# Attention over a long cache: dealing each head's keys to partitions in runs of 512 instead of runs of 128 per piece

## The chip, the cores and the metric

One core of one Trainium2 chip. The metric is the device time of one execution in microseconds (us). Runs of one call share a chip and the runs of the kernel before. A ratio below is the mean time of one kernel's fast runs over the mean of the other's fast runs of the same rounds, so it isn't quite the ratio of the medians quoted beside it. A run counts as slow when its time is more than 1.5% above the fastest of the same kernel.

## The reference

One token attends to a cache of 65,536 keys in each of 32 heads. A small gated feed-forward network runs beside it and the two results are mixed.

```python
B, Sq, D = 1, 1, 512
H, Sk, Dh = 32, 65536, 128            # k_cache, v_cache: [1, 32, 65536, 128] bf16, 512 MB each
q = (x @ wq).reshape(B, Sq, H, Dh)    # (transposed to heads first)
scores = einsum("bhqd,bhkd->bhqk", q, k_cache) * Dh ** -0.5
o = einsum("bhqk,bhkd->bhqd", softmax(scores), v_cache)
a = o.reshape(B, Sq, H * Dh) @ wo
b = (silu(x @ w_gate) * (x @ w_up)) @ w_down
g = sigmoid((x * gate_w).sum(-1))
out = g * a + (1 - g) * b
```

## The kernel before

K and V stream once through a ring of four slots of 4 MB (32 KB in each of 128 partitions). A head of 16 MB is four pieces. `kv_src` says which bytes of the cache make up piece `i`, and in it lies the whole change.

```python
P = 128; GB = 8; CB_MAX = 128; NSLOT = 4; SHARE = 4     # CB = 128 keys per partition and piece, NCH = 4 pieces per head

def kv_src(t, i):
    h, c = divmod(i, NCH)
    return t[0, h, c * CB * P:(c + 1) * CB * P, :].rearrange("(p r) d -> p (r d)", p=P)

# ... one queue (SyncE) issues every large load, as soon as its slot is free:
def load(eng, w, job):
    i = place[job]
    if i >= NSLOT:
        for cond in free_of(jobs[i - NSLOT]):
            w(*cond)
    for n, (dst, src) in enumerate(pieces(job)):
        done = ld[i % NSLOT]
        # ...
        eng.dma_start(dst, src).then_inc(done, 16)
```

The use of a piece doesn't depend on which keys it holds. Three quarters of a K piece go through TensorE (transpose, copy by ScalarE, product with q), and one quarter through VectorE (product with a broadcast q, then a sum). A V piece is multiplied by the matching column of probabilities. The source lines named in the profile are marked.

```python
# TensorE, K:
last = nc.tensor.transpose(dst[:, k * 128:(k + 1) * 128], src[:, b * 128:(b + 1) * 128], ident[:])   # L535
# ScalarE:
nc.scalar.activation(KT[:, g % NKT, :], kt_ps(g), ACT.Copy, bias=0.0)                                # L345
# TensorE, scores:
last = mm(psS[:, c % 2, col:col + 1], KT[:, g % NKT, k * 128:(k + 1) * 128], qc[...])                # L548
# VectorE, the last quarter of the piece:
nc.vector.tensor_tensor(prod[:], kb, qb, ALU.mult)                                                   # L424
# TensorE, V: partition p and block b of V meet partition p and column b of the probabilities
last = mm(psO[:, c % 2, 0:1], src[:, b * 128:(b + 1) * 128], p_of(c)[:, b:b + 1], ...)               # L566
```

Of the kernel before, what the change touches and what calls it, by code (L numbers as in the profile page):

```python
# [5 lines left out]
P = 128  # L6
# [21 lines left out]
def bass_gated_mix__mha_block_cached__swiglu_ffn__decode_kernel(  # L28
# [21 lines left out]
    CB = min(CB_MAX, NC_H)  # L50
# [14 lines left out]
    with ExitStack() as ctx:  # L65
# [55 lines left out]

        def kv_src(t, i):
            h, c = divmod(i, NCH)
            return t[0, h, c * CB * P:(c + 1) * CB * P, :].rearrange("(p r) d -> p (r d)", p=P)

        jobs = [("wq", i) for i in range(NQW)]
        for s in range(NK):
# [27 lines left out]
        def pieces(job):  # L155

            kind, i = job
            if kind == "wq":
                return [(w_q(i), wq_dram[:, i * CQ:(i + 1) * CQ, :])]
            if kind == "wg":  # L160
                return [(by_rows(w_gate()), wg_dram)]
            if kind == "wu":
                return [(by_rows(w_up()), wu_dram)]
            if kind == "wgu":
                return [(by_rows(w_gate()), wg_dram), (by_rows(w_up()), wu_dram)]
            if kind == "wd":
                return [(w_down(), wd_dram)]
            src = kv_src(A_k_cache if kind == "k" else A_v_cache, i)
            dst = flat(job)[:, 0:CB * 128]
            if job == ("v", NK - 1):  # L170
                cut = (CB - TAIL) * 128
                return [(dst[:, 0:cut], src[:, 0:cut]), (dst[:, cut:], src[:, cut:])]
            return [(dst, src)]
# [502 lines left out]
```

## Time and profile before

| | before |
|---|---|
| time, first three runs | 2563.17 us median (2563.04 to 2563.19) |
| span in the profile | 2563.3 us |
| busy: TensorE / ScalarE / VectorE | 72% / 58% / 49% |
| load queue's packets, share of the 16 DMA engines' span | 98.8% |
| 32 KB packets, counted from the trace's DMA records | 32,768; median 1214 ns, mean 1223.8 ns |
| of these over 1273 ns | 670 |

These are lines of the profile page of the kernel before. First comes the span. The DMA and GB/s lines cut the span into 40 equal slices, with the busy share in tenths and the rate. Then come the load queue (packets, MB, share of 16 engines), the chain of work that ended last, three groups of instructions (busy us, mean ns of one, then idle time before them and what ended it), and the two kinds of large load (KB each, median us from issue to landing).

```profile
span 2563.3 us, 88371 instructions
...
DMA  9999999999999999999999999999999999999996
GB/s 403 423 425 432 432 431 431 430 431 430 433 430 432 430 431 433 430 433 429 433 429 431 433 426 431 430 432 427 426 425 418 431 429 427 423 422 426 422 419 297
...
q1 hardware_dynamic: 37874, 1083.46, 98.8%
...
DMA 67%; PE 13%; ACT 11%; issue 9%; POOL 0%; DVE 0%; ACTq 0%; SPq 0%; POOLq 0%; DVEq 0%
DMA ring<-in_A_k_cache_dram 66%; ACT KT L345 10%; PE psT L535 9%; PE psS L548 2%; PE psO L566 1%; ACT pcol L325 1%; DMA ring<-in_A_wq_dram 1%; PE psT L596 0%; PE psT L515 0%; POOL amx L304 0%; PE psS L508 0%; PE psO L589 0%; DVE mxs L441 0%; ACTq L205 0%; DVE sS L434 0%
...
L345 ACT ACTIVATE KT<-psT 128x1024 bf16<-128x1024 bf16 x1536 | 1443.0, 1039 | 972.7 <-PE psT L535 969.8
L535 PE MATMUL psT<-ident,ring 128*128 128x128 bf16 x12288 | 1138.7, 255 | 527.6 <-DMA ring<-in_A_k_cache_dram 525.5
...
L424 DVE TENSOR_TENSOR prod<-ring,qbc 128x2048 f32<-128x2048 bf16 x256 | 586.7, 2292 | 592.1 <-DMA ring<-in_A_k_cache_dram 586.7
...
ring<-in_A_k_cache_dram SPq DMA_DIRECT2D x128, 4096.0 KB, 28.0
ring<-in_A_v_cache_dram SPq DMA_DIRECT2D x127, 4096.0 KB, 33.7
```

The DMA engines are full in every slice but the last, and what the chain follows back is mostly K loads. The first instructions on a K piece (L535, L424) are idle over 500 us waiting for it. By contrast, ScalarE's idle time is spent on TensorE. So the loads bound the kernel.

A 4 MB load takes some 28 to 34 us from issue to landing, yet one completes every 4.19 MB / 430 GB/s = 9.8 us. About three are in the queue together, so the issue of a load isn't what costs.

The packet records size this. Nearly every packet is one row of 32 KB. The 5th and the 50th percentile are 1213 and 1214 ns, so there is a floor: 32,768 B / 1213 ns = 27.0 GB/s per engine, 432 GB/s for 16, within 1 GB/s of the best slice of the page (433). The Trainium skill, "HBM Reference", section "Specifications (TRN2)", says that a core streaming alone gets about 425 GB/s, bounded by its 16 DMA engines. This trace agrees, with 425 GB/s over the span.

### The profile page before, as it was taken

How to read it: one execution, taken by the hardware profiler on the slowest of the kernel's cores; microseconds unless marked ns; L12 is line 12 of the kernel's file. 1: busy time of each engine (PE TensorE's matmuls, PEld its weight loads, DVE VectorE, ACT ScalarE, POOL GpSimd, SP SyncE). 2: the span in 40 equal slices, each digit the busy share in tenths (PEclk: the TensorE clock that was granted, in tenths of full speed). 3: DMA queues.
4: the chain of work that ended last, by engine and by line, in shares of the span. 5: the costliest groups of instructions: out<-in, count | busy, mean ns of one | idle time of the engine just before them, and what ended most of it. 6: DMA issues, size and time to landing. Idle time of an engine off the chain costs nothing.

```text
span 2563.3 us, 88371 instructions
## 1 busy us (share of the span) xinstructions
PE 1848.0 (72%) x41279; PEld 1701.2 (66%) x41280; DVE 1259.2 (49%) x953; ACT 1484.7 (58%) x1799; POOL 42.3 (2%) x72
## 2 busy tenths in 40 slices
PE   6877777777777767776777677777766776777766
PEld 4777666666666666666766666666666666666665
DVE  2754554554455445544554454455444544455441
ACT  3766665566556655655665566556655665566552
POOL 0000000000000000000000000000000000000000
PEclk8778776777767767777676677777777777777776
DMA  9999999999999999999999999999999999999996
GB/s 403 423 425 432 432 431 431 430 431 430 433 430 432 430 431 433 430 433 429 433 429 431 433 426 431 430 432 427 426 425 418 431 429 427 423 422 426 422 419 297
DMA packets 42053, 1088.43 MB, mean 425 GB/s; under 512 B 4481, under 2 KB 8578, under 8 KB 8706
## 3 DMA queue, kind: packets, MB, share of 16 engines
q1 hardware_dynamic: 37874, 1083.46, 98.8%
q10 hardware_dynamic: 4112, 4.19, 0.5%
q8 instruction: 27, 0.44, 0.1%
q14 instruction: 40, 0.33, 0.0%
HBM read 1087.64 MB, written 0.00 MB: 424 GB/s over the span
## 4 chain that ended last, share of the span: by engine, by line
DMA 67%; PE 13%; ACT 11%; issue 9%; POOL 0%; DVE 0%; ACTq 0%; SPq 0%; POOLq 0%; DVEq 0%
DMA ring<-in_A_k_cache_dram 66%; ACT KT L345 10%; PE psT L535 9%; PE psS L548 2%; PE psO L566 1%; ACT pcol L325 1%; DMA ring<-in_A_wq_dram 1%; PE psT L596 0%; PE psT L515 0%; POOL amx L304 0%; PE psS L508 0%; PE psO L589 0%; DVE mxs L441 0%; ACTq L205 0%; DVE sS L434 0%
## 5 line engine op out<-in xcount | busy, mean ns | idle before, releaser
L345 ACT ACTIVATE KT<-psT 128x1024 bf16<-128x1024 bf16 x1536 | 1443.0, 1039 | 972.7 <-PE psT L535 969.8
L535 PE MATMUL psT<-ident,ring 128*128 128x128 bf16 x12288 | 1138.7, 255 | 527.6 <-DMA ring<-in_A_k_cache_dram 525.5
L535 PEld LDWEIGHTS psT<-ident,ring 128*128 128x128 bf16 x12288 | 912.3, 116 | 538.3 <-DMA ring<-in_A_k_cache_dram 271.7
L424 DVE TENSOR_TENSOR prod<-ring,qbc 128x2048 f32<-128x2048 bf16 x256 | 586.7, 2292 | 592.1 <-DMA ring<-in_A_k_cache_dram 586.7
L548 PE MATMUL psS<-qc,KT 128*128 128x1 bf16 x12288 | 550.8, 166 | 139.9 <-ACT KT L345 92.7
L548 PEld LDWEIGHTS psS<-qc,KT 128*128 128x128 bf16 x12288 | 467.7, 100 | 257.7 <-ACT KT L345 252.5
L426 DVE TENSOR_REDUCE sS<-prod 128x16 f32<-128x2048 f32 x256 | 585.2, 2286 | 8.7
L566 PE MATMUL psO<-pcol,ring 128*128 128x1 bf16 x16384 | 475.7, 164 | 19.9 <-issue 9.2
L566 PEld LDWEIGHTS psO<-pcol,ring 128*128 128x128 bf16 x16384 | 450.4, 99 | 24.0 <-issue 14.6
L434 DVE COPY sS<-psS 128x96 f32<-128x96 f32 x128 | 33.0, 257 | 607.2 <-PE psS L548 607.2
L325 ACT ACTIVATE pcol<-sS,nbias 128x128 bf16<-128x128 f32 x128 | 52.3, 408 | 41.7 <-POOL nbias L306 41.6
L304 POOL PARTITION_ALL_REDUCE amx<-mxs x32 | 16.1, 502 | 2137.5 <-DVE mxs L441 2137.5
L445 DVE COPY oparts<-psO 128x1 f32<-128x1 f32 x127 | 18.9, 149 | 25.2 <-PE psO L566 25.1
L306 POOL TENSOR_SCALAR nbias<-amx 128x1 f32<-128x1 f32 x32 | 24.5, 767 | 333.6 <-issue 333.6
L325 ACT ACTIVATION_READ_ACCUMULATOR pcol<-sS,nbias 128x1 f32 x128 | 26.1, 204 | 0.0
L380 DVE COPY qc<-qTb 128x1 bf16<-128x1 bf16 x128 | 19.9, 156 | 4.4
L441 DVE TENSOR_REDUCE mxs<-sS 128x1 f32<-128x512 f32 x32 | 21.7, 677 | 0.0
L332 ACT ACTIVATE qbc<-psT 128x512 bf16<-128x512 f32 x4 | 2.4, 597 | 23.1 <-PE psT L515 23.1
L596 PE MATMUL psT<-wo_sb,oTn 128*1 128x512 bf16 x31 | 11.2, 540 | 5.6 <-DVE oTn L476 5.6
L508 PE MATMUL psS<-xT,ring 128*128 128x1 bf16 x128 | 3.6, 165 | 12.3 <-DMA ring<-in_A_wq_dram 12.3
L508 PEld LDWEIGHTS psS<-xT,ring 128*128 128x128 bf16 x128 | 3.5, 104 | 12.4 <-issue 12.4
L596 PEld LDWEIGHTS psT<-wo_sb,oTn 128*1 128x1 bf16 x31 | 3.3, 110 | 12.7 <-issue 11.7
(44 smaller groups left out, 43.2 us busy)
## 6 DMA issues: line engine op xcount, KB each, us to landing
ring<-in_A_k_cache_dram SPq DMA_DIRECT2D x128, 4096.0 KB, 28.0
ring<-in_A_v_cache_dram SPq DMA_DIRECT2D x127, 4096.0 KB, 33.7
wo_sb<-in_A_wo_dram ACTq DMA_DIRECT2D x1, 4096.0 KB, 157.0
ring<-in_A_wq_dram SPq DMA_DIRECT2D x1, 4096.0 KB, 17.6
ring<-in_A_v_cache_dram SPq DMA_DIRECT2D x1, 3584.0 KB, 34.6
ring<-in_B_w_gate_dram SPq DMA_DIRECT2D x1, 1792.0 KB, 31.3
ring<-in_B_w_up_dram SPq DMA_DIRECT2D x1, 1792.0 KB, 35.5
ring<-in_B_w_down_dram SPq DMA_DIRECT2D x1, 1792.0 KB, 39.7
```

What stands on the lines that cost most here:

```text
L306: nc.gpsimd.tensor_scalar_mul(nbias[:, h:h + 1], amx[:, h:h + 1], -SCALE).then_inc(sm["s_nb"], 1)
L325: nc.scalar.activation(p_of(c), sS[:, h % NS, j * CB:(j + 1) * CB], ACT.Exp, bias=nbias[:, h:h + 1], scale=SCALE, accum_out=rsum[:, c:c + ...
L345: nc.scalar.activation(KT[:, g % NKT, :], kt_ps(g), ACT.Copy, bias=0.0).then_inc(sm[ev_of(g)[0]], 1)
L380: nc.vector.tensor_copy(qc[:, c % 2:c % 2 + 1], qTb[:, c // NCH:c // NCH + 1]).then_inc(sm[cq_of(c)[0]], 1)
L424: nc.vector.tensor_tensor(prod[:], kb, qb, ALU.mult).then_inc(sm["s_tt"], 1)
L426: nc.vector.reduce_sum(sS[:, h % NS, cc * CB + b0:cc * CB + b0 + DB], prod[:], AX_X).then_inc(sm["s_rd"], 1)
L434: nc.vector.tensor_copy(sS[:, h % NS, cc * CB:cc * CB + CBT], psS[:, c % 2, 0:CBT]).then_inc(sm["s_rc"], 1)
L441: nc.vector.reduce_max(mxs[:, h:h + 1], sS[:, h % NS, :], AX_X).then_inc(sm["s_mx"], 1)
L445: nc.vector.tensor_copy(oparts[:, c:c + 1], psO[:, c % 2, 0:1]).then_inc(sm[oc_of(c)[0]], 1)
L535: last = nc.tensor.transpose(dst[:, k * 128:(k + 1) * 128], src[:, b * 128:(b + 1) * 128], ident[:])
L548: last = mm(psS[:, c % 2, col:col + 1], KT[:, g % NKT, k * 128:(k + 1) * 128], qc[:, c % 2:c % 2 + 1], start=True, stop=True)
L566: last = mm(psO[:, c % 2, 0:1], src[:, b * 128:(b + 1) * 128], p_of(c)[:, b:b + 1], start=(b == 0), stop=(b == CB - 1))
```

## The change

The intent is another layout of a head. Partition p holds keys 512p to 512p+511 of the head in all, and a piece is a 32 KB column of that. The rows of a piece lie 128 KB apart in memory instead of 32 KB, and a piece spreads over 16 MB instead of one contiguous 4 MB.

```diff
         def kv_src(t, i):
             h, c = divmod(i, NCH)
-            return t[0, h, c * CB * P:(c + 1) * CB * P, :].rearrange("(p r) d -> p (r d)", p=P)
+            return t[0, h].rearrange("(p r) d -> p (r d)", p=P)[:, c * CB * 128:(c + 1) * CB * 128]
```

K and V use the same function, so their keys are permuted alike. A softmax followed by a weighted sum doesn't depend on the order of the keys.

## The prediction

> **What bounds the kernel now.** The loads. The page's DMA line is 9 (90% or more) in 39 of 40 slices, mean 425 GB/s; in the DMA queue table the load queue's packets take 98.8% of the 16 engines' span. The chain of waits is 66% K loads. Compute has slack: PE 72%, ScalarE 58%, VectorE 49%; in the waits, the first transposes of a piece wait 525.5 us in total for K loads. The table of issues gives 28.0 and 33.7 us from issue to landing for K and V pieces of 4 MB, while one lands about every 9.8 us (4.19 MB at 430 GB/s): about three transfers are queued, and no issue time is exposed.
>
> By packet (the trace's DMA records): the ring's loads are almost all 32 KB packets, one per partition row, 32,768 of them. The median takes 1214 ns, the 5th and 25th percentiles both 1213: a flat floor of 27 GB/s per engine, 432 GB/s for 16. Only about 670 packets take over 60 ns more, the worst 3.45 us; together they cost about 17 us per engine (estimate: summed excess over 16), mostly in the last third. At the floor everything takes about 2,505 us of engine time; the rest of the 2,563 us is start (about 8 us), slow packets, the engines' uneven finish (about 2,534 to 2,549 us, reconstructed) and a closing chain of about 14 us.
>
> **What the change does.** It adds and removes no instruction; the order on every engine is the same. Partitions hold runs of 512 keys of a head instead of 128 per piece. Softmax and the weighted sum ignore the order of keys, and K and V are permuted alike. Bytes, packet count and packet size stay. Only source addresses move: the row pitch goes from 32 KB (a piece is one contiguous 4 MB) to 128 KB (128 runs spread over 16 MB; the four pieces of a head interleave).
>
> **On the critical path.** All of it: each packet is on the bounding resource. If a packet stays at its 1213 ns, nothing changes. The floor is equal for nearly all packets, which looks like a limit of the DMA engine, not of the memory, so little is to be gained: with every slow packet gone, 15 to 35 us (about 1%).
>
> The risk is memory contention. The Trainium skill, "DMA: Bandwidth & Descriptors", section "Latency and other measured facts", reports copies within HBM of 16 KiB rows: a pitch of 512 KiB gave 207 GB/s per direction against 214 at full rate, 2 MiB gave 164, 4 MiB 103. 128 KB lies below these, so the loss should be under its 3%; my estimate from that page is 0 to 1%. No trace here shows it yet: every large load of this kernel is of contiguous pieces.
>
> **Predicted time: 2567 us, 8 in 10 between 2550 and 2597 us.** Faster by over 2%: 0.01; within 2%: 0.90; slower by over 2%: 0.09.
>
> **What would show it.** Right: median 32 KB packet still 1213 to 1215 ns, queue share near 99%, GB/s per slice 420 to 433, chain of waits unchanged, busy times of PE, ScalarE and VectorE within 1%; only the number of slow packets moves, between half and three times the 670. Wrong: a median above about 1235 ns, or 2,000 or more slow packets; then GB/s drops evenly, issue-to-landing rises, and the transposes' wait for K grows by the whole loss.
>
> **What would make it wrong.** Power-of-two starts of the 16 engines (several rows apart, so now hundreds of KB to megabytes) meeting in the same memory channels in lockstep: several per cent. In the other direction, if the slow packets come from the contiguous layout, up to 1% comes back.

## The result, and the profile after

| | before | after |
|---|---|---|
| time, 4 runs each | 2563.11 us median (2558.77 to 2563.19) | 2561.74 us median (2560.60 to 2565.64) |
| ratio of fast runs, 95% interval | | 1.0002 (0.9984 to 1.0019) |
| 32 KB packets: median, mean | 1214, 1223.8 ns | 1214, 1221.9 ns |
| over 1273 ns | 670 | 560 |

The lines of the page of the kernel after that answer to those shown of before:

```profile
span 2558.7 us, 88371 instructions
...
DMA  9999999999999999999999999999999999999997
GB/s 403 422 428 431 431 430 432 431 431 430 432 431 431 431 431 432 431 431 430 430 433 430 429 434 427 428 432 429 429 427 430 430 427 425 416 424 432 427 426 299
...
q1 hardware_dynamic: 37874, 1083.46, 98.8%
...
DMA 67%; PE 12%; ACT 11%; issue 9%; POOL 0%; DVE 0%; ACTq 0%; SPq 0%; POOLq 0%; DVEq 0%
DMA ring<-in_A_k_cache_dram 66%; ACT KT L345 10%; PE psT L535 8%; PE psS L548 2%; ACT pcol L325 1%; PE psO L566 1%; DMA ring<-in_A_wq_dram 1%; PE psT L596 0%; PE psT L515 0%; POOL amx L304 0%; PE psS L508 0%; PE psO L589 0%; DVE mxs L441 0%; ACTq L205 0%; DVE sS L434 0%
...
L345 ACT ACTIVATE KT<-psT 128x1024 bf16<-128x1024 bf16 x1536 | 1443.1, 1042 | 973.5 <-PE psT L535 970.7
L535 PE MATMUL psT<-ident,ring 128*128 128x128 bf16 x12288 | 1129.3, 253 | 532.3 <-DMA ring<-in_A_k_cache_dram 530.9
...
L424 DVE TENSOR_TENSOR prod<-ring,qbc 128x2048 f32<-128x2048 bf16 x256 | 586.7, 2292 | 598.5 <-DMA ring<-in_A_k_cache_dram 593.1
...
ring<-in_A_k_cache_dram SPq DMA_DIRECT2D x128, 4096.0 KB, 28.1
ring<-in_A_v_cache_dram SPq DMA_DIRECT2D x127, 4096.0 KB, 33.7
```

Nothing moved. The packet count and the share of the queue are the same, the chain has the same loads at 66%, and the same groups wait as long as before (530.9 against 525.5 us at L535). The slices agree within a few GB/s. The profiled runs differ by 4.6 us. The packets account for nearly all of that: (1223.8 - 1221.9) ns x 32,768 / 16 = 3.9 us. But the kernel before alone ranged over 4.4 us in its own four runs, so this difference is noise and not an effect of the layout.

### The profile page after: what moved, and what is told of

It is laid out like the page before. It is cut to its first block, busy times and chain, and to the rows that moved or that the text cites. A ratio compares the mean times of both kernels' runs of the same rounds, so it can differ in the third digit from the quotient of the medians.

```text
span 2558.7 us, 88371 instructions
## 1 busy us (share of the span) xinstructions
PE 1840.4 (72%) x41279; PEld 1688.9 (66%) x41280; DVE 1259.4 (49%) x953; ACT 1483.4 (58%) x1799; POOL 36.0 (1%) x72
## 3 DMA queue, kind: packets, MB, share of 16 engines
q1 hardware_dynamic: 37874, 1083.46, 98.8%
## 4 chain that ended last, share of the span: by engine, by line
DMA 67%; PE 12%; ACT 11%; issue 9%; POOL 0%; DVE 0%; ACTq 0%; SPq 0%; POOLq 0%; DVEq 0%
DMA ring<-in_A_k_cache_dram 66%; ACT KT L345 10%; PE psT L535 8%; PE psS L548 2%; ACT pcol L325 1%; PE psO L566 1%; DMA ring<-in_A_wq_dram 1%; PE psT L596 0%; PE psT L515 0%; POOL amx L304 0%; PE psS L508 0%; PE psO L589 0%; DVE mxs L441 0%; ACTq L205 0%; DVE sS L434 0%
## 5 line engine op out<-in xcount | busy, mean ns | idle before, releaser
L535 PE MATMUL psT<-ident,ring 128*128 128x128 bf16 x12288 | 1129.3, 253 | 532.3 <-DMA ring<-in_A_k_cache_dram 530.9
L535 PEld LDWEIGHTS psT<-ident,ring 128*128 128x128 bf16 x12288 | 905.1, 115 | 543.1 <-DMA ring<-in_A_k_cache_dram 272.5
L306 POOL TENSOR_SCALAR nbias<-amx 128x1 f32<-128x1 f32 x32 | 18.2, 569 | 328.9 <-issue 328.9
```

Source lines behind the costliest of these rows:

```text
L306: nc.gpsimd.tensor_scalar_mul(nbias[:, h:h + 1], amx[:, h:h + 1], -SCALE).then_inc(sm["s_nb"], 1)
```

## The experiments

A null result has two readings. The memory side may not matter at all (theory A). Or it matters for large power-of-two distances, and 128 KB is short of them (rival B). The experiments widen the distance, then ask what it is about the distance that hurts.

Eleven of the twelve runs are of kernels that read other bytes than they should; the twelfth is of the changed kernel itself. Apart from half_v, which loads less, they move the same number of bytes in rows of the same size, and only the staggered one adds loads. The check is blind to which keys a piece holds, and "correct" for the changed kernel doesn't prove its permutation. That rests on the argument about K and V above.

This table sums up the runs. The last two columns are counted from the DMA records of each profiled run, for the packets of 32 KB.

| run | rows apart | median us (lowest to highest) | ratio to before | packets: mean ns | over 1273 ns |
|---|---|---|---|---|---|
| after_again | 128 KB | 2561.24 (2559.06 to 2561.88) | 0.9995 (0.9982 to 1.0009) | 1221.6 | 471 |
| pitch_512k | 512 KB | 2561.15 (2559.41 to 2563.79) | 0.9996 (0.9979 to 1.0013) | 1221.5 | 530 |
| pitch_2m | 2 MB | 2572.82 (2568.65 to 2575.66) | 1.0037 (1.0018 to 1.0057) | 1224.7 | 1058 |
| pitch_4m | 4 MB | 2772.24 (2725.42 to 2797.72) | none given | 1318.3 | 8524 |
| pitch_4m_again | 4 MB | 2695.88 (2684.26 to 2718.79) | 1.0551 (1.0513 to 1.0590) | 1282.0 | 5704 |
| pitch_4m_less_4k | 4 MB - 4 KB | 2560.49 (2559.41 to 2562.01) | 0.9992 (0.9976 to 1.0009) | 1222.6 | 559 |
| pitch_4m_staggered | 4 MB | 2687.37 (2684.48 to 2702.26) | 1.0510 (1.0478 to 1.0543) | 1278.4 | 5842 |
| pad_in_engine | 4 MB - 4 KB in fours, fours 16 MB apart | 2655.42 (2652.41 to 2662.42) | 1.0369 (1.0352 to 1.0386) | 1268.8 | 4566 |
| pad_between_engines | 4 MB in fours, fours 16 MB - 16 KB apart | 2562.33 (2561.55 to 2562.71) | 1.0001 (0.9985 to 1.0016) | 1223.3 | 625 |
| pitch_0 | 0 | 2559.67 (2558.66 to 2561.38) | 0.9996 (0.9980 to 1.0013) | 1222.1 | 482 |
| reversed | 32 KB | 2561.18 (2559.55 to 2565.54) | 1.0006 (0.9989 to 1.0022) | 1221.7 | 444 |
| half_v | 32 KB | 2222.91 (2219.89 to 2225.68) | 0.8677 (0.8663 to 0.8692) | not comparable | not comparable |

### The changed kernel again: after_again

No edit.

> The changed kernel itself, in more rounds, to narrow the interval: the theory that a 32 KB packet at a 128 KB pitch keeps its 1213 ns asks for a ratio of 0.999 to 1.001 to before. A ratio outside 0.998 to 1.002 would mean a small effect that the first rounds hid.

Measured: 0.9995 (0.9982 to 1.0009). The ratio lies within what theory A asked for. With both sets of rounds, an effect of the change over 0.2% in either direction is outside the intervals.

### Wider pitches: pitch_512k, pitch_2m, pitch_4m

A piece now takes its rows from `m` pieces' worth of memory, whatever head they belong to.

```diff
-            h, c = divmod(i, NCH)
-            return t[0, h, c * CB * P:(c + 1) * CB * P, :].rearrange("(p r) d -> p (r d)", p=P)
+            m = 16                          # 64 for 2 MB, 128 for 4 MB
+            w = CB * Dh
+            a = t.rearrange("b h s d -> (b h s d)")[i // m * m * P * w:(i // m + 1) * m * P * w]
+            return a.rearrange("(p x) -> p x", p=P)[:, i % m * w:(i % m + 1) * w]
```

> Wrong result on purpose: a piece mixes four heads, so that rows of 32 KB lie 512 KB apart; instructions, bytes and packets are those of before. Theory A (each DMA engine moves 32 KB in 1213 ns whatever the memory does, and the memory has room to spare): median packet 1213 to 1215 ns, time within 0.5% of before, 2550 to 2575 us. Rival B (the memory begins to conflict at large power-of-two pitches, and 128 KB is just short of it): packets lengthen, 3% or so more time, 2600 to 2680 us, with thousands of packets over 1273 ns.

> Wrong result on purpose: rows 2 MB apart. Theory A: no change, 2550 to 2575 us. Rival B: what the Trainium skill (DMA: Bandwidth & Descriptors, Latency and other measured facts) reports for copies, 164 against 214 GB/s, carried over to loads would be 2563 x 214/164 = 3340 us; a load makes only half the memory traffic of a copy at the same rate per direction, so less is possible: 2650 to 3400 us, median packet over 1300 ns.

> Wrong result on purpose: rows 4 MB apart, the largest pitch that the cache holds. Theory A: no change, 2550 to 2575 us, median packet 1213 to 1215 ns. Rival B: up to 2563 x 214/103 = 5300 us by the page's figures for copies; at the least over 2800 us, and the whole increase is found as waits for loads, with compute busy times unchanged.

At 512 KB there is no effect. Its page has the span and the load queue of before:

```profile
span 2558.1 us, 88372 instructions
...
q1 hardware_dynamic: 37874, 1083.46, 98.8%
```

At 2 MB the time rises by 0.4%, inside theory A's range of times but clear of 1.0 in its interval. The long packets rise from some 500 to 1058. At 4 MB theory A falls. Rival B's sizes fall too, since it asked for at least 2650 and 2800 us. Three of the four runs at 4 MB count as slow, because they are over 1.5% above the fastest of the same kernel. That is this kernel's own spread, as the kernel before on the same chip stayed within 2558 to 2566 us in all runs. No verdict is taken from these; the next run has four fast ones. Its page, span and slices:

```profile
span 2764.9 us, 88372 instructions
...
GB/s 321 279 309 332 361 383 396 412 427 426 413 408 425 432 422 407 408 421 414 404 396 395 408 416 404 396 417 422 416 399 386 402 404 412 398 405 417 419 381 253
```

### The 4 MB pitch on another chip: pitch_4m_again

> The 4 MB pitch once more, as the control of the two padded versions on their own chip: 2700 to 2810 us, lowest GB/s in the first slices, if the first runs are representative. If it is near 2563 us here, the slowness belonged to the chip of the first runs.

The median is 2696 us, just under the expected range, and the ratio is 1.055. The slowness is not one chip's, but its size differs: 5.5% here, and 8.2% by the medians of the first (2772.24 / 2563.22). The page of this run, span, slices and load queue:

```profile
span 2682.5 us, 88372 instructions
...
GB/s 345 306 343 367 390 377 370 419 425 425 409 411 428 429 429 424 424 432 431 428 415 416 427 429 421 414 422 428 428 416 404 419 421 421 410 414 431 432 392 259
...
q1 hardware_dynamic: 37874, 1083.46, 99.0%
```

The load queue is as full as before (99.0%), but the slices start at 345, 306 and 343 GB/s and recover to 424 to 432 by the middle. The median packet is still 1213 ns; what grows is a tail, from 670 to 5704 packets over 1273 ns. About half of those (2842) are in the first quarter of the packets; the other quarters have 644, 961 and 1257, so the slowness fades and then comes back in part.

The mean packet accounts for the loss: (1282.0 - 1223.8) ns x 32,768 / 16 = 119 us, and the profiled spans differ by 2682.5 - 2563.3 = 119 us. Most of it, 107 of the 119 us, arrives where a bound by loads must put it, at the transposes' wait for K. This is that line of the list of waits (total us, times, longest us), first of the kernel before, then of this run (the same instruction is on L537 here):

```profile
PE psT L535 <- DMA ring<-in_A_k_cache_dram: 525.5, 118, 5.3
```

```profile
PE psT L537 <- DMA ring<-in_A_k_cache_dram: 632.9, 125, 10.6
```

### Power of two or wide spread: pitch_4m_less_4k

```diff
+            w = CB * Dh
+            pitch = 128 * w - 2048           # 2048 elements of 2 bytes: 4 MB less 4 KB
+            a = t.rearrange("b h s d -> (b h s d)")[0:P * pitch].rearrange("(p x) -> p x", p=P)
+            first = min(i * w, pitch - w)
+            return a[:, first:first + w]
```

> Wrong result on purpose: rows 4 MB minus 4 KB apart, so the span of addresses is that of the 4 MB pitch but the starts of the rows do not agree in their low bits. Both theories: 2550 to 2575 us; if the 4 MB pitch is slow and this one is not, the cause is the power of two, and if both are slow, it is the wide spread of the addresses (rival C).

The ratio is 0.9992. The pieces spread over the same 512 MB, and no time is lost. This was run on the same chip as the 4 MB pitch that lost 8%. So the cause is the equal low address bits of the rows, not the spread. Span and slices, to be held against those of the 4 MB pitch above:

```profile
span 2557.9 us, 88372 instructions
...
GB/s 403 422 430 430 430 432 431 432 429 433 432 428 433 430 430 432 432 431 431 431 430 432 430 429 432 431 430 429 422 426 428 429 427 427 420 430 434 429 426 302
```

### Which rows must not agree: pad_in_engine, pad_between_engines

The rows of one DMA are shared out over 16 engines, each taking some rows one after the other. The Trainium skill, "DMA: Bandwidth & Descriptors", section "The descriptor swizzle", gives the split: eight rows each, in two groups of four neighbours. The trace doesn't record the engine of a packet, so no run here shows the split. The experiment is built to hold for groups of four and of eight. In both kernels the last piece is loaded as before. The cut shows the new lines of both kernels together, each ending in its own `return`.

```diff
+            w = CB * Dh
+            pitch = 128 * w
+            a = t.rearrange("b h s d -> (b h s d)")
+            first = min(i * w, pitch - w - 8192)
+            # pad_in_engine: 4 KB less between rows of a group, groups of four exactly 16 MB apart
+            return bass.AP(a.tensor, a.offset + first, [[4 * pitch, P // 4], [pitch - 2048, 4], [1, w]])
+            # pad_between_engines: the complement
+            return bass.AP(a.tensor, a.offset + first, [[4 * pitch - 8192, P // 4], [pitch, 4], [1, w]])
```

> Wrong result on purpose: as the 4 MB pitch, but within each group of four successive rows the pitch is 4 MB minus 4 KB, while the 32 groups start at exact multiples of 16 MB. Whichever way rows are dealt to engines (groups of four or of eight), engines working in step then read different addresses with equal low bits. Theory L (it is the addresses that different engines read at one time): the padding is of no use, 2680 to 2810 us, first slices near 300 GB/s. Rival (the rows that one engine reads one after the other must not be at equal low bits): as fast as before, 2550 to 2575 us.

> Wrong result on purpose: the complement. Within each group of four rows the pitch is exactly 4 MB; the groups start at multiples of 16 MB minus 16 KB, as in the version with 4 KB off every row. Theory L: 2550 to 2575 us, under 1000 packets over 1273 ns. Rival: slow, 2680 to 2810 us.

Both ran on the chip of pitch_4m_again. Their span and slices, first with the padding inside the groups, then between them:

```profile
span 2653.2 us, 88372 instructions
...
GB/s 348 334 360 384 383 402 410 427 428 428 420 424 424 432 426 420 426 429 426 419 417 413 423 427 420 419 423 423 413 410 409 420 422 431 419 421 428 428 410 282
```

```profile
span 2559.7 us, 88372 instructions
...
GB/s 403 424 426 430 432 430 429 433 431 427 434 432 429 432 433 428 432 433 428 431 433 431 428 430 432 427 432 427 425 431 427 428 424 420 427 426 434 427 427 296
```

Padding between the groups gives back all of the 134 us (2695.88 - 2562.38), although the rows within a group still lie exactly 4 MB apart. Padding within the groups leaves 93 us (2655.42 - 2562.38) of the loss. It gave back 40 us, which theory L had not expected, and its time falls below the expected range. With the split that the page gives, the rival (an engine's own successive rows) is refuted. That rows read by different engines must not agree fits both runs, but they don't isolate it. The paddings differ in size (4 KB steps against 16 KB steps), and in how many different offsets the 128 rows of a piece have (4 against 32), so that the number or the size of the offsets is a rival which no run tests. Why padding within the groups helps a third is open too. Engines that stand a row apart would meet at different paddings, which fits, but no run tests it.

### Timing between engines: pitch_4m_staggered

To the 4 MB pitch this adds 15 small loads into a slot that is not in use yet, and a wait before that slot is filled.

```diff
+            rows = A_wq.rearrange("(p c) n -> p (c n)", p=P)
+            for n in range(15, 0, -1):
+                sp.dma_start(ring[0:n, 3, n * 1024:(n + 1) * 1024],
+                             rows[0:n, n * 1024:(n + 1) * 1024]).then_inc(sm["s_st"], 16)
             for job in jobs:
+                if place[job] == 3:
+                    w("s_st", 15 * 16)
                 load(sp, w, job)
```

> Wrong sums on purpose: the 4 MB pitch, after 15 small loads of 15, 14, ... 1 rows of 2 KB, meant to give each of the 16 DMA engines 2 KB (some 76 ns at 27 GB/s) more to do than the next before the large loads begin, so that they do not walk the low address bits in step. Theory L (the 4 MB pitch is slow while the engines read equal low address bits at the same time): the first eight slices, 279 to 412 GB/s without the stagger, come to 380 GB/s or more, and the time falls below 2720 us. Rival (rows at this pitch conflict whatever the engines' timing): the first slices stay near 300 GB/s and the time near 2770 us.

The time (2687 us) is below 2720 us, but the slices are not what was expected:

```profile
span 2684.0 us, 88386 instructions
...
GB/s 325 310 334 380 400 400 399 429 426 430 424 425 430 427 429 418 428 428 429 417 415 421 420 411 413 411 424 429 414 407 409 426 426 420 396 404 415 428 396 252
```

The first three (325, 310, 334) are as low as without a stagger. The run was made on another chip than either control, and the controls differ by 76 us from each other, so 9 us below the lower of them says nothing. The experiment is inconclusive. The starts of the packets in the DMA records say why: the edit didn't do what it was meant to. The first K piece begins with the 129th to the 144th of the 32 KB packets. In the staggered kernel 14 of these 16 start within 171 ns of each other, in the two controls within 757 and 1197 ns. The small loads brought the engines together instead of 76 ns apart each, and by 60 us after the first packet nothing of it is left: the packets in flight had started between 126 and 1733 ns before.

The same records speak against the idea behind it, that the engines start in step within their rows and drift apart. In pitch_4m_again, 60 us after the first 32 KB packet, in the slow stretch, the 16 packets in flight had started between 82 and 1943 ns before; at 1200 us, where the slices are over 420, between 24 and 1143 ns before. The engines were all over their rows from the start. So why the slow slices come first is open. In all these kernels a later piece also lies further along in the 4 MB, so the place in the rows may matter and not the time; no run reads the 4 MB pitch in another order.

### The same row for all: pitch_0

```diff
+            w = CB * Dh
+            a = t.rearrange("b h s d -> (b h s d)")[i * w:(i + 1) * w]
+            return a.unsqueeze(0).broadcast_to([P, w])
```

> Wrong result on purpose: every partition reads the same 32 KB of a piece, so the engines touch 1/128 of the addresses, all at the same low bits. If the 1213 ns per 32 KB is the DMA engine's own rate and equal addresses are served from what is open already: 2550 to 2575 us. If what counts is engines meeting at equal low address bits (as at the 4 MB pitch), it is at least as slow as that one: 2750 us or more, with over 8000 packets above 1273 ns.

```profile
span 2556.8 us, 88371 instructions
...
q1 hardware_dynamic: 37874, 1083.46, 98.9%
```

There is no loss and no gain. Equal low bits alone don't slow the engines, provided that the whole address is equal as well; different addresses that agree in their low bits do. And 128 engine reads of the same 32 KB are no faster than reads of 4 MB, with the median packet again at 1214 ns. This supports the engine's own rate as the floor.

### Where the few long packets come from: reversed

```diff
-            h, c = divmod(i, NCH)
+            h, c = divmod(NK - 1 - i, NCH)
```

> Wrong result on purpose: contiguous pieces as before, but read from the last head to the first. Time unchanged, 2555 to 2570 us. Of before's 671 packets over 1273 ns, 185 fell in the first half of the run and 486 in the second. If the slow packets belong to addresses, the halves change places; if to the time in the run (engines that have drifted apart), they stay.

(The 671 there count one smaller packet; of 32 KB there are 670. Split at 1277 us from the first packet, they are 199 and 471.) Read in the opposite order, the counts are 187 and 257. The halves don't change places, so the excess of before isn't tied to addresses. Nor is it a property of the kernel. The same split gives 179 and 381 for the first profile of the changed kernel, and 187 and 284 for the second. The first half repeats within about 20, and the second half differs from run to run. What makes those packets long is open; all of them together cost each engine some 12 to 17 us of 2560 (their excess over 1214 ns, summed and divided by 16, in reversed and in before).

### How close compute is behind: half_v

```diff
+            if kind == "v":
+                return [(dst[:, 0:CB * 64], src[:, 0:CB * 64])]
             return [(dst, src)]
```

> Wrong result on purpose: of each V piece but the last only half is loaded (16 KB per row), 266 MB of 1088 less; compute unchanged. If the loads are all that bounds: 817 MB at 432 GB/s plus some 45 us of start and end, 1915 to 1970 us. If compute is close behind (PE 1848 us busy): 2000 to 2200 us. If compute or waits bounded already: near 2563 us.

The time is 2223 us, above both ranges. Its span, load queue and chain of work that ended last:

```profile
span 2222.4 us, 88371 instructions
...
q1 hardware_dynamic: 37874, 817.12, 88.6%
...
PE 40%; issue 32%; ACT 21%; POOL 4%; DMA 2%; DVE 2%; ACTq 0%; POOLq 0%; SPq 0%; DVEq 0%
ACT KT L347 19%; PE psO L568 17%; PE psT L537 15%; PE psS L550 6%; POOL amx L306 3%; ACT pcol L327 2%; DMA ring<-in_A_k_cache_dram 1%; DVE mxs L443 1%; DMA ring<-in_A_wq_dram 1%; PE psT L598 0%; DVE sS L436 0%; POOL nbias L308 0%; PE psT L517 0%; PE psS L510 0%; ACTq L207 0%
```

A quarter of the bytes is gone and only 13% of the time. The chain holds 2% of DMA instead of 67%: TensorE, ScalarE and the issue time between them bound now. So the loads did bound the kernel before, but compute stands about 13% behind them, nearer than TensorE's 72% of busy time suggests. (The granted clock was 0.76 to 0.77 here and 0.73 to 0.74 in the runs of before; the margin at before's clock was not measured.) The table calls the packets not comparable because the queue runs dry here: of the 507 packets of 32 KB that started with at most ten in flight, 477 took over 1273 ns, at rows 32 KB apart. So a tail of long packets alone doesn't prove a conflict of addresses.

## Why the prediction was right

- **Bound by loads: shown.** The page, and half_v (less to load, less time) and the 4 MB pitch (longer packets, as much more time) on both sides of it.
- **No instruction, byte or packet changes: shown.** Instructions 88,371 and packets 37,874 in both pages.
- **The packet's floor of 1213 ns doesn't depend on the address: shown.** Every layout, even the slow ones, has a median of 1213 or 1214 ns. What can grow is the tail of long packets. Of the prediction's signs of failure, a median above 1235 ns and an even drop of GB/s would have missed the 4 MB slowness, with its median of 1213 ns and its slow start; the count of long packets finds it.
- **Little to gain: not contradicted.** No layout is faster than before outside noise, down to reading one row 128 times. The 15 to 35 us named for removing the long packets was not tested, as none of the runs removed them.
- **Risk of 0 to 1%, from the skill's page on copies: too high in size.** It measured 0.0% (within 0.2%). The predicted 2567 us is 5 us above the measured median, presumably by this term. Loads here lose far less than the page's copies at the same pitch: nothing at 512 KB, 0.4% at 2 MB, 5.5 to 8% at 4 MB.
- **The signs in the profile: all but one as written.** The chain, queue share, median packet and busy times held, and the long packets went from 670 to 560. The range of 420 to 433 GB/s per slice was too narrow: leaving out the start and the end, the page of after has a 416 and a 434, and the page of before already had a 418 and a 419.
- **"Power-of-two starts in the same memory channels in lockstep": half shown.** Agreement of rows in their low bits is real and costs time at 4 MB. That it is the rows of different engines fits the two padded runs, which don't isolate it. That channels are what they meet in is not shown by any run. Lockstep within the rows is not what the trace shows, with starts spread over 82 to 1943 ns in the slow stretch.

## What to carry to other kernels

When the profile shows full DMA queues and nearly every packet at one floor, a change that only moves the source addresses of rows of the same size has little to win (here, no layout won anything), and the question is only whether it lengthens packets. For the 32 KB rows of this kernel on one core it did not at pitches of 128 and 512 KB, did by 0.4% at 2 MB and by 5% or more at 4 MB; there, 4 KB less between all rows, or 16 KB less between groups of four, restored the full rate. Where attention is averaged over so many keys, a passing check doesn't prove that a permutation is right, so argue it from the code or test it with other inputs.

## What the Trainium skill lacked or had wrong

- "DMA: Bandwidth & Descriptors", section "Latency and other measured facts", row pitch at large powers of two: it has figures only for copies within HBM of 16 KiB rows (207, 164 and 103 against 214 GB/s at 512 KiB, 2 MiB and 4 MiB). Loads of 32 KB rows into SBUF lose much less: ratios in time of 0.9996 at 512 KB, 1.0037 at 2 MB and 1.055 at 4 MB (8% by the medians on another chip). It lacks a case for loads.
- The same row says that 4 KB of padding restores the full rate. The runs agree (0.9992 with 4 KB less per row). It doesn't say where the padding must be: with 16 KB between groups of four rows all of it comes back (1.0001), with 4 KB between the rows within them only a third does (1.0369, against 1.0551 without any).
- The same row calls the mechanism an inference. The runs add that the slowness is greatest at the start (345, 306, 343 GB/s in the first three of 40 slices) and fades to 424 to 432 by the middle, that the engines were not in step within their rows while it lasted (starts 82 to 1943 ns before one instant), and that reading one and the same row for all partitions costs nothing (0.9996).
- No page gives the time of a 32 KB packet of a load, only a rate for a whole engine. Here it is 1213 ns at the floor and 1213 or 1214 at the median, 27.0 GB/s per engine, in every layout.
